# Banded attention with a mixture layer: PSUM tiles of one bank each, and GpSimd as the issuer of most later transfers

## The chip, the cores and the metric

The kernel runs on one core of one Trainium2 chip. The metric is the device time of one execution in microseconds (us). The kernel before took 714.76 us, the median of 3 runs (714.32 to 716.55). The profile is of one further execution, which took 713.8 us.

Five engines work side by side, each through its own list of instructions in a fixed order: PE (TensorE, matrix products), DVE (VectorE), ACT (ScalarE), POOL (GpSimd) and SP (SyncE, which here only issues transfers). An instruction starts when those before it in its own list are out of the way and the semaphores that it waits for have arrived. Products land in PSUM, which has eight banks of 512 fp32 numbers per partition.

## What is computed

Attention with a window and a few sink positions, then two dense layers with a gate between them, all in fp32:

```python
keep = is_sink | in_window                  # 4 sinks, a window of 128
scores = np.where(keep, scale * np.matmul(q, k.transpose(0, 1, 3, 2)), -1e9)
a = softmax(scores)
x = np.matmul(a, v)                         # 4 x 8 heads x 768 x 64
x = x.transpose(0, 2, 1, 3).reshape(3072, 512)
h = x @ w_in                                # 512 -> 2048
out = (h - np.tanh(h)) @ w_out              # 2048 -> 512
```

## The kernel before

**Tiling.** The 3072 tokens are cut into 12 chunks of 256. A chunk's attention is four units (a unit is two heads), so there are 48. A chunk's dense part is eight steps, one for each group of 256 hidden columns, so there are 96. Products are made in fp32r with operands split into a high and a low part, so that a product takes three passes (high by high, low by high, high by low).

**A unit.** The scores (L511, or L504 in the first 12 units) go into a pair of PSUM banks, one bank for each head. `merge` (L516 to L534) copies the sink columns into place under a mask (`copy_predicated`, L525) and then masks and finds the extreme of a row (L531). Exponentials and scales follow on ACT (L539, L565), sums on DVE (L559, L560), small copies for the sinks on POOL (L574 to L576). `turn` transposes the probabilities on PE into bank t (L599); ACT copies them out (L616, or L606 for the first chunk of a sequence), DVE writes a masked copy (L613), POOL masks the other (L619). `attend` transposes the sink columns into bank x (L640), ACT copies them (L647), and PE multiplies with the values (L656, L662) into banks x and t, from which ACT and DVE make the high and low part of x (L674, L678). Ahead of all that, `split` makes high and low parts of the keys (L469 on ACT, L474 on DVE) and of the queries (L479 on ACT, L482 on POOL).

**A step.** 24 products (L777) make two halves of h in one of two further PSUM buffers. The gate is tanh on ACT (L796) and a difference on DVE (L799). In chunks 3 and 4 and in the last step, high and low of it (L802, L805) go into 12 products with w_out (L847). In chunks 5 to 11 the second layer is one level of Strassen's scheme: sums on DVE (L810 to L812), high and low (L815 on ACT, L818 on DVE), and 21 products (L881) into seven accumulators that lie in the banks s0, s1, o0 and o1. At a chunk's end `gather` adds these up (L920 on ACT, L924 to L933 on DVE) and the result is stored (L938). `derive` (L964 to L1030) makes the summed weights for it during chunks 3 and 4. The last chunk's last step puts its products (L847) into banks t and x, which L953 adds.

**Weights.** w_in is spilled to a scratch in DRAM, `wscr`. From chunk 3 on each step reads its 1 MB of w_in again as four blocks into a ring of five buffers (`ring` and `spare`, L762). One part of w_out is put away in `kscr` and read back near the end (L742).

**Order.** No loop order is written down. Each piece of work is given to `Work.add` with an engine, an assumed duration, a due time, and the resources that it reads and writes; `Work.order` then runs a list scheduler over all of it, which picks, whenever an engine comes free, the ready piece with the earliest due time. The instructions of each engine are issued in that order. The due times come from constants (`PACE` for the distance of steps, `LEAD` for how far a chunk's attention lies ahead of its steps, `STREAM` for the ring loads, and others). The planner knows single banks (its resources are "s0", "s1", "o0", "o1", "t", "x"). The tiles of the language, which decide on what an instruction really waits, were three: `sbank`, `obank` and `txbank`, of two banks each.

**Transfers.** All of them are issued by SP, in one list.

Of the kernel before, what the change touches and what calls it, by code (L numbers as in the profile page):

```python
# [18 lines left out]
P = 128  # L19
# [213 lines left out]
def _banded(tc, qd, kp, vp, vs, masks, w_in, w_out, ident, pts, early, out):  # L233
    nc = tc.nc
    et = mybir.EngineType
    with ExitStack() as ctx:
# [26 lines left out]
        SLK, PAD, LATE, QP, KP, BP, LEAD3 = 0.0, 1.05, 65222.0, 1, 0, 1, 37045.0  # L263
# [56 lines left out]
        def load_qk(u):  # L320
# [34 lines left out]
            work.add("SP", 500, t, keys, (), [slots(u)[0], "seq k"], lands=800)  # L355
            work.add("SP", 1000, t, queries, (), [slots(u)[1], "seq q"], lands=600 if raw(u) else 1000)
# [3 lines left out]
        def load_v(cc):  # L360
            b, c = chunks[cc]
            first = max(0, 2 * c - 1)
            if c and chunks[cc - 1] == (b, c - 1):
                first = 2 * c
                if c:
                    vslot[cc, first - 1] = vslot[cc - 1, first - 1]
            new = range(first, 2 * c + 2)
            for i in new:
                vslot[cc, i] = ("v", len(vnew) % 3)
                vnew.append(i)  # L370

# [8 lines left out]
            work.add("SP", 500 * took, due_unit(4 * cc), values, (), [vslot[cc, i] for i in new] + ["seq v"],  # L380
                     lands=1000 * took)
# [111 lines left out]
        def scores(u, t):  # L493
# [4 lines left out]
            def products():  # L498
                both = obank if apart else sbank if cc <= SA else txbank
                ps = [both[:, h, :] for h in range(2)]  # L500
                sps[u, t] = both, ps
# [14 lines left out]
            def merge():  # L516
                both, ps = sps[u, t]
# [220 lines left out]
        def keep(back):  # L738
            for f in range(2):
                a = wt[1, NG - 1][:, :, f, (1 - f) * DM // 2 : (2 - f) * DM // 2].bitcast(F32)  # L740
                if back:
                    nc.sync.dma_start(a, kscr[f])  # L742
# [93 lines left out]
        def sums_of(n, cc, t):  # L836
            return (sbank, txbank, obank)[{1: 0, 2: 1, NCHUNK - 1: 1}.get(cc, 2)][:, t, :]

        def mm2(n, k):
# [16 lines left out]
            4: (sbank[:, 0, :HALF], 1), 3: (sbank[:, 0, HALF:], 0), 1: (obank[:, 1, :HALF], 2),  # L856
            2: (sbank[:, 1, :HALF], 3), 5: (sbank[:, 1, HALF:], 4),
            7: (obank[:, 0, :HALF], 6), 6: (obank[:, 0, HALF:], 5),
# [51 lines left out]
        def gather(n):  # L910
# [8 lines left out]
            def copy():  # L919
                nc.scalar.copy(v, pair(sbank[:, 0, :]))  # L920

            def add1():
                one = obank[:, 1, :HALF].unsqueeze(1).to_broadcast([P, 2, HALF])
                nc.vector.tensor_tensor(u, one, v, op=ALU.add)  # L924

            def add2():
                nc.vector.tensor_tensor(v, pair(sbank[:, 1, :]), v, op=ALU.add)
                for k in range(2):
                    nc.vector.tensor_tensor(u[:, k, :], u[:, k, :], sbank[:, 1, (1 - k) * HALF : (2 - k) * HALF], op=ALU.subtract)

            def add3():
                for k in (1, 0):
                    nc.vector.tensor_tensor(u[:, k, :], obank[:, 0, k * HALF : (k + 1) * HALF], u[:, k, :], op=ALU.add)  # L933
# [12 lines left out]
            if cc < NCHUNK - 1:  # L946
                for t in range(2):
                    work.add("SP", 500, d + 1000, lambda t=t: put(t), o, (), lands=1000)
                return

            def add4(t):
                part = four[:, 0::3, :] if t else four[:, 1:3, :]
                nc.vector.tensor_tensor(part, pair(txbank[:, t, :]), part, op=ALU.add)  # L953
# [172 lines left out]
        for n in range(NS):  # L1126
# [6 lines left out]
            if n:  # L1133
# [8 lines left out]
                if n - 1 == order.index((NCHUNK - 2, NG - 1)):  # L1142
                    work.add("SP", 1000, due_step(n + 2), lambda: keep(True), ["kept"], [("w", 1, NG - 1)], lands=2050)
# [214 lines left out]
```

## Time and profile before

| | |
|---|---|
| median of 3 runs | 714.76 us |
| profiled execution | 713.8 us |
| its span (first to last instruction) | 712.0 us |
| PE busy | 94% of the span |
| DVE busy | 77% |
| ACT busy | 58% |
| POOL busy | 25% |

The span is what the trace shows; 1.8 us of the execution lie around it. A busy share is an average over stages that differ: the first 80 us (loading, decoding weights, the first three chunks' attention), 80 to 200 us (plain steps of chunks 0 to 2), 200 to 360 us (chunks 3 and 4, with the derivation of Strassen's weights), 360 to 640 us (chunks 5 to 10 with attention beside them), and the rest. Where the trace gives a wait, it names what came last by semaphore.

### The profile page before, as it was taken

The numbers are of one execution on the slowest core, as the hardware profiler recorded it, in microseconds if no ns is written. First come the engines' busy times: TensorE is split into PE (matmuls) and PEld (weight loads), VectorE is DVE, ScalarE is ACT, GpSimd is POOL, SyncE is SP. The second block draws the span as 40 slices with busy tenths as digits, with TensorE's granted clock in tenths as the row PEclk, the third lists the DMA queues.
The fourth block names the chain that finished last, engine by engine and source line by source line (L and its number), as shares of the span: only waits on it lengthen the run. The fifth ranks groups of instructions, "written<-read, shape, count | busy, mean of one in ns | idle before, by whom it ended". The sixth has DMA issues, their size and how long they took to land.

```text
span 712.0 us, 14370 instructions
## 1 busy us (share of the span) xinstructions
PE 666.9 (94%) x5099; PEld 611.2 (86%) x5099; DVE 551.4 (77%) x1305; ACT 410.0 (58%) x1056; POOL 177.2 (25%) x287
## 2 busy tenths in 40 slices
PE   6788999999999997999999999999999998999896
PEld 5556899889988787889889889999999998999895
DVE  6777998964878898889878768877886876875554
ACT  5876333345876675656567557566565665663231
POOL 5332100001436464313222212223111231210000
PEclk9999999999999998999999999999999999999999
DMA  6769972432148665657857865866775775664761
GB/s 187 244 198 335 351 293 104 152 115 86 53 116 242 187 194 155 194 161 232 229 178 200 258 185 174 239 211 190 232 220 185 210 239 167 180 184 135 237 192 65
DMA packets 77485, 137.23 MB, mean 193 GB/s; under 512 B 8156, under 2 KB 28764, under 8 KB 77404
## 3 DMA queue, kind: packets, MB, share of 16 engines
q1 hardware_dynamic: 77404, 136.22, 62.0%
q8 instruction: 42, 0.69, 0.4%
q14 instruction: 39, 0.32, 0.1%
HBM read 120.98 MB, written 15.20 MB: 191 GB/s over the span
## 4 chain that ended last, share of the span: by engine, by line
PE 71%; DVE 10%; DMA 7%; ACT 6%; issue 2%; POOL 1%; SPq 0%; ACTq 0%; DVEq 0%
PE h L777 30%; PE sbank L881 10%; PE obank L881 7%; DMA ring<-wscr 6%; PE txbank L662 5%; PE obank L847 5%; PE txbank L847 3%; PE sbank L847 3%; PE txbank L511 3%; PE txbank L599 2%; DVE pt L613 2%; PE sbank L511 1%; ACT p L565 1%; PE txbank L656 1%; ACT pt L616 1%
## 5 line engine op out<-in xcount | busy, mean ns | idle before, releaser
L777 PE MATMUL h<-xh,ring 128*128 128x256 f32 x924 | 185.8, 282 | 8.6 <-DMA ring<-wscr 5.5
L777 PEld LDWEIGHTS h<-xh,ring 128*128 128x128 f32 x924 | 151.3, 190 | 10.9 <-DMA ring<-wscr 7.0
L777 PE MATMUL h<-xl,ring 128*128 128x256 f32 x462 | 129.0, 279 | 0.0
L796 ACT ACTIVATE gbuf<-h 128x512 f32<-128x512 f32 x96 | 57.3, 597 | 105.5 <-PE h L777 65.8
L482 POOL TENSOR_TENSOR q<-qraw,q 128x512 fp32r<-128x512 f32 x36 | 47.4, 1318 | 254.5 <-ACT q L479 254.5
L777 PEld LDWEIGHTS h<-xl,ring 128*128 128x128 f32 x462 | 87.6, 190 | 0.4
L539 ACT ACTIVATE p<-p,st 128x132 f32<-128x132 f32 x168 | 66.5, 398 | 26.8 <-DVE st L531 25.6
L815 ACT CAST ghbuf<-gbuf 128x896 fp32r<-128x896 f32 x55 | 51.9, 943 | 39.1 <-DVE gbuf L812 38.7
L777 PE MATMUL h<-xh,w 128*128 128x256 f32 x384 | 73.4, 281 | 0.0
L818 DVE TENSOR_TENSOR glbuf<-gbuf,ghbuf 128x896 fp32r<-128x896 f32 x55 | 61.2, 1112 | 15.2 <-ACT ghbuf L815 13.6
L777 PEld LDWEIGHTS h<-xh,w 128*128 128x128 f32 x384 | 60.8, 188 | 1.3 <-PE txbank L662 0.2
L565 ACT ACTIVATE p<-p,st 128x132 f32<-128x132 f32 x168 | 54.2, 394 | 4.3 <-DVE st L560 3.8
L474 DVE TENSOR_TENSOR ks<-kraw,ks 64x392 fp32r<-64x392 f32 x72 | 49.5, 687 | 5.6 <-ACT ks L469 3.0
L777 PE MATMUL h<-xl,w 128*128 128x256 f32 x192 | 53.5, 279 | 0.0
L847 PE MATMUL obank<-w,ghbuf 128*128 128x512 f32 x192 | 51.5, 399 | 1.4 <-ACT ghbuf L802 1.4
L799 DVE TENSOR_TENSOR gbuf<-h,gbuf 128x512 f32<-128x512 f32 x55 | 37.9, 689 | 18.8 <-ACT gbuf L796 18.3
L777 PE MATMUL h<-xh,spare 128*128 128x256 f32 x228 | 50.7, 285 | 0.2 <-DMA spare<-wscr 0.2
L619 POOL TENSOR_TENSOR pt<-pt,after 128x512 f32<-128x512 f32 x32 | 43.4, 1358 | 29.4 <-ACT pt L616 27.3
L613 DVE TENSOR_TENSOR pt<-txbank,below 128x512 f32<-128x512 f32 (+1 forms) x48 | 28.9, 602 | 26.8 <-ACT pt L616 9.7
L574 POOL CAST z<-p 128x16 fp32r<-128x16 f32 x42 | 11.5, 274 | 124.4 <-ACT p L565 119.2
L662 PE MATMUL txbank<-pt,v 128*64 128x128 f32 (+1 forms) x512 | 41.5, 315 | 0.0
L662 PEld LDWEIGHTS txbank<-pt,v 128*64 128x64 f32 x512 | 31.0, 137 | 11.8 <-issue 4.6
(157 smaller groups left out, 1620.8 us busy)
## 6 DMA issues: line engine op xcount, KB each, us to landing
ring<-wscr SPq DMA_DIRECT2D x231, 256.0 KB, 4.1
spare<-wscr SPq DMA_DIRECT2D x57, 256.0 KB, 4.1
qraw<-qd SPq DMA_DIRECT2D x36, 256.0 KB, 4.6
wraw<-w_in SPq DMA_DIRECT2D x16, 512.0 KB, 8.2
wraw<-w_out SPq DMA_DIRECT2D x16, 512.0 KB, 8.2
wscr<-w SPq DMA_DIRECT2D x16, 512.0 KB, 4.9
kraw<-kp SPq DMA_DIRECT2D x38, 196.0 KB, 3.9
v<-vp SPq DMA_DIRECT2D x27, 256.0 KB, 2.9
```

What stands on the lines that cost most here:

```text
L474: (nc.gpsimd if KP else nc.vector).tensor_tensor(k[o, h, :], t[r, :], k[r, h, :].bitcast(F32), op=ALU.subtract)
L482: (nc.gpsimd if QP else nc.vector).tensor_tensor(ql[u], qt[u], qh[u].bitcast(F32), op=ALU.subtract)
L539: nc.scalar.activation(e, e, AF.Exp, bias=st[u][:, j : j + 1], scale=-1.0, accum_out=st[u][:, 4 + j : 5 + j],)
L565: nc.scalar.activation(pr[u][:, j, :], pr[u][:, j, :], AF.Copy, scale=s[:, 8 + j : 9 + j])
L619: nc.gpsimd.tensor_tensor(w[:, :, 0, :], w[:, :, 0, :], after.unsqueeze(1).to_broadcast([P, 4, P]), op=ALU.mult)
L662: nc.tensor.matmul(xps[key][(p - p0) // 2][h * 64 : h * 64 + 64, p % 2, a:z], lhsT=vt[cc, i][:, hd : hd + D], rhs=rhs, start=False, stop=p ...
L777: nc.tensor.matmul(hps[n][:, f, :], lhsT=w, rhs=x, start=r == 0, stop=r == 11)
L796: nc.scalar.activation(g0, h(), AF.Tanh)
L815: nc.scalar.copy(ghbuf[:, n % 2], gbuf[:, 1:, :])
L818: nc.vector.tensor_tensor(glbuf[:, :7, :], gbuf[:, 1:, :], ghbuf[:, n % 2].bitcast(F32), op=ALU.subtract)
L847: nc.tensor.matmul(sums_of(n, cc, t), lhsT=a[:, f, t * P : (t + 1) * P], rhs=wt[1, g][:, (0, 1, 0)[i], f, :], start=first and not low and ...
L881: nc.tensor.matmul(acc, lhsT=a[:, b, :], rhs=factor(g, m, part % 2), start=g == 0 and part == 0 and m in (4, 1, 2, 7), stop=closes(n) and ...
```

## The change

Four things are changed.

1. The three PSUM tiles of two banks become six tiles of one bank. A `copy_predicated` over two banks becomes two, one per bank, each ahead of its own head's masking.
2. From chunk 4 on the values, from unit 12 on the keys and queries, the output stores of chunks 5 to 10, and the reload of `kscr` are issued by GpSimd: 104 transfers (36 of keys, 36 of queries, 18 of values, 12 stores, 2 of `kscr`). SP's list falls from 701 to 597 instructions.
3. `QP` goes from 1 to 0: the low part of the queries (L482, 36 instructions) is made by VectorE.
4. Eight constants of the planner change.

The instructions of PE are the same in number; VectorE gets 116 more (36 and 80).

```diff
-        sbank = ps.tile([P, 2, 512], F32, tag="s", name="sbank")
-        obank = ps.tile([P, 2, 512], F32, tag="o", name="obank")
-        txbank = ps.tile([P, 2, 512], F32, tag="tx", name="txbank")
-        tbank, xbank = txbank[:, 0, :], txbank[:, 1, :]
+        banks = {n: ps.tile([P, 512], F32, tag=n, name=n) for n in ("s0", "s1", "o0", "o1", "t", "x")}
+        sbank, obank, txbank = ((banks[a], banks[b]) for a, b in (("s0", "s1"), ("o0", "o1"), ("t", "x")))
+        tbank, xbank = txbank
...
-        SLK, PAD, LATE, QP, KP, BP, LEAD3 = 0.0, 1.05, 65222.0, 1, 0, 1, 37045.0
+        SLK, PAD, LATE, QP, KP, BP, LEAD3 = 0.0, 1.05, 65222.0, 0, 0, 1, 32490.0
...
-        FIRST, EARLY, PACE, LEAD = 45000.0, 4600.0, 7980.0, 43356.0
+        FIRST, EARLY, PACE, LEAD = 45000.0, 4600.0, 7895.0, 33530.0
...
-        HALF2, LAST = 8253.0, 6188.0
-        SPILL, STREAM, DEAR, DLATE = 36773.0, 5446.0, 120000.0, 17426.0
+        HALF2, LAST = 8807.0, 174.0
+        SPILL, STREAM, DEAR, DLATE = 25023.0, 6494.0, 120000.0, 31436.0
...
-                nc.sync.dma_start(kt[u], kp[b, p, :, 2 * c * TS : 2 * c * TS + KW])
+                (nc.sync if raw(u) else nc.gpsimd).dma_start(kt[u], kp[b, p, :, 2 * c * TS : 2 * c * TS + KW])
...
-                    nc.sync.dma_start(qt[u], src.rearrange("h d s -> d h s"))
+                    nc.gpsimd.dma_start(qt[u], src.rearrange("h d s -> d h s"))
...
-                    nc.sync.dma_start(vt[cc, i], vp[b, i * P : (i + 1) * P, :])
+                    (nc.sync if cc < 4 else nc.gpsimd).dma_start(vt[cc, i], vp[b, i * P : (i + 1) * P, :])
...
-                if kind > 0:
-                    nc.vector.copy_predicated(
-                        both[:, :, TS:WIN], above.bitcast(U32).unsqueeze(1).to_broadcast([P, 2, P]),
-                        both[:, :, :P],
-                    )
                 for h in range(2):
+                    if kind > 0:
+                        nc.vector.copy_predicated(ps[h][:, TS:WIN], above.bitcast(U32), ps[h][:, :P])
...
-                nc.sync.dma_start(out[r0 : r0 + P, :].rearrange("p (k c) -> p k c", k=2), src)
+                (nc.gpsimd if cc < NCHUNK - 1 else nc.sync).dma_start(
+                    out[r0 : r0 + P, :].rearrange("p (k c) -> p k c", k=2), src
+                )
```

Three places show how the lists change. The names at the end of a row are tiles, with a running number where there are several; line numbers of the kernel after are smaller by two to five than those of before.

The first place is the issuing of the last chunk's values. Before, SP issued them between ring loads:

```order
L377 DMA v_4_6932<-vp 128x512
L377 DMA v_5_6934<-vp 128x512
L762 DMA ring<-wscr 128x512
L762 DMA spare<-wscr 128x512
L343 DMA qraw_7028<-qd 128x2x256
L762 DMA ring<-wscr 128x512 x4
L762 DMA spare<-wscr 128x512
L762 DMA ring<-wscr 128x512
L334 DMA kraw_7107<-kp 128x392
```

In the kernel after, POOL issues the same values:

```order
L333 DMA kraw_7033<-kp 128x392
L377 DMA v_4_7049<-vp 128x512
L377 DMA v_5_7051<-vp 128x512
L342 DMA qraw_7140<-qd 128x2x256
L570 CAST z<-p_7086 128x2x8
L571 TENSOR_TENSOR z<-p_7086,z 128x2x8
L572 CAST z<-z 128x2x16
L333 DMA kraw_7197<-kp 128x392
L615 TENSOR_TENSOR pt<-pt,after 128x4x128
L934 DMA out<-wide 128x512
L934 DMA out<-wide 256x1x256
```

Keys, values, queries and stores have moved from among SP's ring loads to among POOL's sink copies (L570 to L572) and masked products (L615); SP there now issues ring and spare loads alone.

The second place is VectorE's list at the end of chunk 6, where `gather` reads the accumulators. Before:

```order
L799 TENSOR_TENSOR gbuf<-h_4980,gbuf 128x512
L810 TENSOR_TENSOR gbuf<-gbuf 128x256
L811 TENSOR_TENSOR gbuf<-gbuf 128x256
L812 TENSOR_TENSOR gbuf<-gbuf 128x128
L613 TENSOR_TENSOR pt<-txbank,below 128x4x128
L924 TENSOR_TENSOR wide<-obank,wide 128x2x256
L927 TENSOR_TENSOR wide<-sbank,wide 128x2x256
L929 TENSOR_TENSOR wide<-wide,sbank 128x256 x2
L933 TENSOR_TENSOR wide<-obank,wide 128x256 x2
L818 TENSOR_TENSOR glbuf<-gbuf,ghbuf 128x896
L525 COPY_PREDICATED txbank<-above,txbank 128x2x128
```

After, at the same place:

```order
L795 TENSOR_TENSOR gbuf<-h_5045,gbuf 128x512
L806 TENSOR_TENSOR gbuf<-gbuf 128x256
L807 TENSOR_TENSOR gbuf<-gbuf 128x256
L808 TENSOR_TENSOR gbuf<-gbuf 128x128
L920 TENSOR_TENSOR wide<-o_239,wide 128x2x256
L923 TENSOR_TENSOR wide<-s_237,wide 128x2x256
L925 TENSOR_TENSOR wide<-wide,s_237 128x256 x2
L929 TENSOR_TENSOR wide<-o_238,wide 128x256 x2
L525 COPY_PREDICATED t<-above,t 128x128
L527 ISA p_5117,st_5118<-t,mask 128x132
L527 ISA st_5118 128x1
L525 COPY_PREDICATED x<-above,x 128x128
```

The additions stand in the same order and now name one bank each (o_239 is o1, s_237 is s1, o_238 is o0); the masked copy before them (L613) is gone from here, and the predicated copy is halved and alternates with the masking (L527).

The third place is VectorE's list where the Strassen weights of group 6 are derived a second time (L985 to L1008 before, L983 to L1006 after). Before:

```order
L985 TENSOR_TENSOR wide<-w_6_1527 128x512
L799 TENSOR_TENSOR gbuf<-h_3627,gbuf 128x512
L613 TENSOR_TENSOR pt<-txbank,below 128x4x128
L810 TENSOR_TENSOR gbuf<-gbuf 128x256
L811 TENSOR_TENSOR gbuf<-gbuf 128x256
L812 TENSOR_TENSOR gbuf<-gbuf 128x128
L987 TENSOR_TENSOR wide<-wide,w_6_1527 128x512
L989 TENSOR_TENSOR wide<-wide,w_6_1527 128x512
L818 TENSOR_TENSOR glbuf<-gbuf,ghbuf 128x896
```

After:

```order
L983 TENSOR_TENSOR wide<-w_6_1554 128x512
L985 TENSOR_TENSOR wide<-wide,w_6_1554 128x512
L987 TENSOR_TENSOR wide<-wide,w_6_1554 128x512
L555 TENSOR_SCALAR st_3812<-st_3812 128x4
L556 RECIPROCAL st_3812<-st_3812 128x4
L482 TENSOR_TENSOR q_3840<-qraw_3593,q_3840 128x512
L1004 TENSOR_TENSOR w_6_1554<-wide,w_6_1554 128x256
L1006 SCALAR_TENSOR_TENSOR w_6_1554<-wide,w_6_1554 128x256
L474 TENSOR_TENSOR ks_3871<-kraw_3614,ks_3871 64x392 x2
```

The low part of the queries (L482) now stands in VectorE's list, and the three sums of the derivation follow one another.

On PE, the last product with the values of a chunk (L662) stood 1.5 to 2.75 steps ahead of the first step of that chunk in chunks 4 to 11; it now stands 0.75 to 2 steps ahead.

## Rows read from the trace of the kernel before

**Rows 1.** The busy time of each engine over the span, with its share and its number of instructions (PEld is the loading of weights into TensorE).
```profile
PE 666.9 (94%) x5099; PEld 611.2 (86%) x5099; DVE 551.4 (77%) x1305; ACT 410.0 (58%) x1056; POOL 177.2 (25%) x287
```
**Rows 2.** The span by stage: stretch and its length in us; busy time and (count) of PE, PEld, DVE, ACT and POOL; the granted clock of PE as a share of the full one; the DMA share; GB/s.
```profile
0.00:80.00 80.00, 63.80 (x386) 48.98 (x387) 60.32 (x210) 53.39 (x184) 29.19 (x78) 1.00 0.76 246
80.00:200.00 120.00, 119.36 (x778) 107.41 (x777) 95.71 (x158) 59.25 (x128) 13.77 (x21) 1.00 0.43 154
200.00:360.00 160.00, 151.54 (x1080) 135.22 (x1080) 139.63 (x322) 103.55 (x285) 66.53 (x84) 0.98 0.65 192
360.00:640.00 280.00, 269.21 (x2332) 259.79 (x2331) 217.18 (x550) 173.97 (x434) 66.27 (x104) 1.00 0.68 204
640.00:712.00 72.00, 62.99 (x532) 59.82 (x530) 38.52 (x69) 19.88 (x29) 1.46 (x1) 0.98 0.52 158
```
**Rows 3.** What PE waited for between 80 and 700 us: total in us, times, the longest.
```profile
PE h L777 <- DMA ring<-wscr: 5.5, 7, 1.8
PE sbank L881 <- DVE wide L929: 4.4, 5, 1.0
PE h L777 <- issue: 3.1, 1, 3.1
PE txbank L640 <- DVE pt L613: 2.4, 4, 1.0
...
PE txbank L640 <- ACT pt L616: 1.0, 1, 1.0
```
**Rows 4.** The same view for the first 80 us.
```profile
PE txbank L599 <- ACT zr L647: 3.9, 3, 1.6
...
PE txbank L599 <- DVE xl L678: 1.5, 3, 0.5
PE txbank L640 <- ACT pt L606: 1.0, 1, 1.0
```
**Rows 5.** What SP's queue waited for between 200 and 700 us, the same columns.
```profile
SPq L377 <- PE txbank L662: 27.4, 8, 5.4
SPq L343 <- POOL q L482: 25.2, 10, 5.9
SPq L334 <- DVE ks L474: 22.3, 21, 2.8
```
**Rows 6.** The timeline around one stop of PE at 601 us: start and duration in us, the instruction, and in brackets the idle time before it with its releaser. Rows of POOL, then SP, then PE.
```profile
596.30 1.29 POOL L482 TENSOR_TENSOR q<-qraw,q 128x512 fp32r<-128x512 f32 x1 [11.29 <-ACT q L479]
...
597.62 0.38 SPq L343 DMA_DIRECT2D qraw<-qd  x1
598.09 2.20 SPq L762 DMA_DIRECT2D ring<-wscr  x4
...
602.95 0.39 PE L777 MATMUL h<-xh,ring 128*128 128x256 f32 x1 [1.85 <-DMA ring<-wscr]
```
**Rows 7.** The timeline at the end of chunk 6, in the same form. Rows of DVE, then PE.
```profile
450.22 0.74 DVE L929 TENSOR_TENSOR wide<-wide,sbank 128x256 f32<-128x256 f32 x2
...
449.52 0.63 PE L511 MATMUL txbank<-ks,q 128*128 128x260 f32 x4
451.11 0.71 PE L881 MATMUL sbank<-edge,ghbuf 128*128 128x256 f32 x4 [0.96 <-DVE wide L929]
...
452.57 0.64 PE L881 MATMUL sbank<-w,ghbuf 128*128 128x256 f32 x4
```
**Rows 8.** Groups of instructions by line and shape over the whole span: out<-in with shapes, count, busy us, mean ns of one, idle time before them. The last row is from the view of one line and gives the least, the median and the greatest duration in ns.
```profile
L482 POOL TENSOR_TENSOR q<-qraw,q 128x512 fp32r<-128x512 f32 x36 | 47.4, 1318 | 254.5 <-ACT q L479 254.5
...
L474 DVE TENSOR_TENSOR ks<-kraw,ks 64x392 fp32r<-64x392 f32 x72 | 49.5, 687 | 5.6 <-ACT ks L469 3.0
...
L805 DVE TENSOR_TENSOR glbuf<-h,ghbuf 128x512 fp32r<-128x512 f32 x41 | 28.1, 685 | 2.5 <-ACT ghbuf L802 2.1
...
L810 DVE TENSOR_TENSOR gbuf<-gbuf 128x256 f32<-128x256 f32 x55 | 24.1, 438 | 1.8
...
L525 DVE COPY_PREDICATED txbank<-above,txbank 128x256 f32<-128x256 uint32 x44 | 18.7, 424 | 9.2 <-PE txbank L511 6.2 <-ACT gbuf L796 2.9
...
L812 DVE TENSOR_TENSOR gbuf<-gbuf 128x128 f32<-128x128 f32 x55 | 17.1, 312 | 1.9
...
L474 DVE TENSOR_TENSOR ks<-kraw,ks x72: 559/562/1418, 153.5 to 625.2; 64x392 fp32r<-64x392 f32 x72
```
**Rows 9.** The longest stop of PE after 80 us, on the timeline (a row of DVE, one of PE), and the stretch in which it lies, in the columns of rows 2.
```profile
280.31 0.68 DVE L805 TENSOR_TENSOR glbuf<-h,ghbuf 128x512 fp32r<-128x512 f32 x1
...
281.09 0.55 PE L777 MATMUL h<-xh,ring 128*128 128x256 f32 x1 [3.14 <-issue]
...
280.00:300.00 20.00, 18.91 (x108) 17.22 (x109) 15.55 (x43) 13.21 (x39) 4.89 (x6) 0.87 0.54 158
```
**Rows 10.** The timeline at the end, DVE.
```profile
705.61 1.29 DVE L953 TENSOR_TENSOR wide<-txbank,wide 128x512 f32<-128x512 f32 x2 [1.29 <-PE txbank L847]
```
**Rows 11.** L482 by stage: stretch, length, busy time of POOL with its count, granted clock, DMA share, GB/s.
```profile
200.00:360.00 160.00, 16.32 (x12) 0.98 0.65 192
360.00:640.00 280.00, 24.64 (x19) 1.00 0.68 204
```
**Rows 12.** L525 by stage, with the busy time and the count of DVE in the same columns.
```profile
200.00:360.00 160.00, 9.73 (x23) 0.98 0.65 192
360.00:640.00 280.00, 15.26 (x36) 1.00 0.68 204
```

More of the change, by code (lines that the diff above doesn't have):

```diff
@@ L354, in load_qk @@
                 work.add("POOL", 460, t - ZL, zeros, (), [slots(u)[1]])
-            work.add("SP", 500, t, keys, (), [slots(u)[0], "seq k"], lands=800)
-            work.add("SP", 1000, t, queries, (), [slots(u)[1], "seq q"], lands=600 if raw(u) else 1000)
+            e = "SP" if raw(u) else "POOL"
+            work.add(e, 500, t, keys, (), [slots(u)[0], "seq k"], lands=800 if raw(u) else 1000)
+            work.add(e, 1000, t, queries, (), [slots(u)[1], "seq q"], lands=600 if raw(u) else 1000)
         vslot, vnew = {}, []
@@ L376, in values @@
                     vt[cc, i] = vpool.tile([P, DM], F32, tag="v", name=f"v{cc}_{i}")
-                    nc.sync.dma_start(vt[cc, i], vp[b, i * P : (i + 1) * P, :])
+                    (nc.sync if cc < 4 else nc.gpsimd).dma_start(vt[cc, i], vp[b, i * P : (i + 1) * P, :])
             took = len(new)
-            work.add("SP", 500 * took, due_unit(4 * cc), values, (), [vslot[cc, i] for i in new] + ["seq v"],
+            work.add("SP" if cc < 4 else "POOL", 500 * took, due_unit(4 * cc), values, (), [vslot[cc, i] for i in new] + ["seq v"],
                      lands=1000 * took)
@@ L499, in products @@
                 both = obank if apart else sbank if cc <= SA else txbank
-                ps = [both[:, h, :] for h in range(2)]
-                sps[u, t] = both, ps
+                ps = sps[u, t] = both
                 for h in range(2):
@@ L516, in merge @@
             def merge():
-                both, ps = sps[u, t]
+                ps = sps[u, t]
                 if t == 0:
@@ L741, in keep @@
                 if back:
-                    nc.sync.dma_start(a, kscr[f])
+                    nc.gpsimd.dma_start(a, kscr[f])
                 else:
@@ L836, in sums_of @@
         def sums_of(n, cc, t):
[L837 removed]
+            return (sbank, txbank, obank)[{1: 0, 2: 1, NCHUNK - 1: 1}.get(cc, 2)][t]
         def mm2(n, k):
@@ L855, in _banded @@
         accs = {
-            4: (sbank[:, 0, :HALF], 1), 3: (sbank[:, 0, HALF:], 0), 1: (obank[:, 1, :HALF], 2),
-            2: (sbank[:, 1, :HALF], 3), 5: (sbank[:, 1, HALF:], 4),
-            7: (obank[:, 0, :HALF], 6), 6: (obank[:, 0, HALF:], 5),
+            4: (sbank[0][:, :HALF], 1), 3: (sbank[0][:, HALF:], 0), 1: (obank[1][:, :HALF], 2),
+            2: (sbank[1][:, :HALF], 3), 5: (sbank[1][:, HALF:], 4),
+            7: (obank[0][:, :HALF], 6), 6: (obank[0][:, HALF:], 5),
         }
@@ L919, in copy @@
             def copy():
-                nc.scalar.copy(v, pair(sbank[:, 0, :]))
+                nc.scalar.copy(v, pair(sbank[0][:, :]))
             def add1():
-                one = obank[:, 1, :HALF].unsqueeze(1).to_broadcast([P, 2, HALF])
+                one = obank[1][:, :HALF].unsqueeze(1).to_broadcast([P, 2, HALF])
                 nc.vector.tensor_tensor(u, one, v, op=ALU.add)
             def add2():
-                nc.vector.tensor_tensor(v, pair(sbank[:, 1, :]), v, op=ALU.add)
+                nc.vector.tensor_tensor(v, pair(sbank[1][:, :]), v, op=ALU.add)
                 for k in range(2):
-                    nc.vector.tensor_tensor(u[:, k, :], u[:, k, :], sbank[:, 1, (1 - k) * HALF : (2 - k) * HALF], op=ALU.subtract)
+                    nc.vector.tensor_tensor(u[:, k, :], u[:, k, :], sbank[1][:, (1 - k) * HALF : (2 - k) * HALF], op=ALU.subtract)
             def add3():
                 for k in (1, 0):
-                    nc.vector.tensor_tensor(u[:, k, :], obank[:, 0, k * HALF : (k + 1) * HALF], u[:, k, :], op=ALU.add)
+                    nc.vector.tensor_tensor(u[:, k, :], obank[0][:, k * HALF : (k + 1) * HALF], u[:, k, :], op=ALU.add)
             def put(t):
@@ L947, in gather @@
                 for t in range(2):
-                    work.add("SP", 500, d + 1000, lambda t=t: put(t), o, (), lands=1000)
+                    work.add("POOL", 500, d + 1000, lambda t=t: put(t), o, (), lands=1000)
                 return
@@ L952, in add4 @@
                 part = four[:, 0::3, :] if t else four[:, 1:3, :]
-                nc.vector.tensor_tensor(part, pair(txbank[:, t, :]), part, op=ALU.add)
+                nc.vector.tensor_tensor(part, pair(txbank[t][:, :]), part, op=ALU.add)
             def end():
@@ L1142, in _banded @@
                 if n - 1 == order.index((NCHUNK - 2, NG - 1)):
-                    work.add("SP", 1000, due_step(n + 2), lambda: keep(True), ["kept"], [("w", 1, NG - 1)], lands=2050)
+                    work.add("POOL", 1000, due_step(n + 2), lambda: keep(True), ["kept"], [("w", 1, NG - 1)], lands=2050)
                 if cc == 0 and g == NG - 1:
```

## The prediction

> **What bounds the kernel now.** I read the busy times first: PE is busy for 666.9 of 712.0 us, DVE for 551.4, POOL for 177.2 [rows 1]. So the end is set by PE's list plus its stops, and an edit pays only where it shortens a stop. The view by stage says where the stops are [rows 2]: PE lacks 80.0 − 63.8 = 16.2 us in the first 80, 0.6 in 80 to 200, 160.0 − 151.5 = 8.5 in 200 to 360, 280.0 − 269.2 = 10.8 in 360 to 640, and 9.0 in the last 72. The reader should also see that DVE is the second engine: 139.6 of 160 us (87%) in the third stage, 217.2 of 280 (78%) in the fourth. Third, PE's waits name who ends the stops [rows 3, 4]: ring loads, DVE's additions at the end of a chunk, copies out of banks t and x. Last, SP's waits show why a ring load comes late: the load ahead of it in the same list waits for a buffer [rows 5].
>
> **Part 1, one tile for each bank.** A wait by the old tile can hold an instruction for a reader of the other bank. The end of chunk 6 is the pattern [rows 7]: the four L881 products that start at 451.11 write bank s0 (accumulators 4 and 3), yet they waited 0.96 us for L929, which reads s1. The first products into s1 start at 452.57, when L929 is done. With six tiles that wait goes. It is there at five chunk ends, 4.4 us in all [rows 3]. Behind it stands only ACT's copy out of s0, which is earlier here. I take 4.0 (bounds 0 and 4.4).
>
> L640 transposes into bank x and waits for L613 and L616, which read bank t: 2.4 + 1.0 = 3.4 us [rows 3]. Behind it stand the small copies that make its input on POOL. I take 2.5 (0 to 3.4).
>
> In the first 80 us L599 (bank t) waits for L647 (bank x) and for L678, which there reads bank x, and L640 (bank x) for L606 (bank t): 3.9 + 1.5 + 1.0 = 6.4 us [rows 4]. Here true waits stand close behind, as the same copies and masks follow each other through both banks in every pair of units. I take about half, 3.0 (0 to 6.4).
>
> At the end both L953 additions wait for the last product, though the first reads bank t only [rows 10]. One of two, 1.29/2 = 0.64 us, can lie beside PE: I take 0.6 (0 to 0.64). Together part 1 gives 4.0 + 2.5 + 3.0 + 0.6 = 10.1 us.
>
> Its cost is on DVE: 80 predicated copies become 160. The shape of 128x256 takes 0.424 us; an addition falls from 0.438 to 0.312 us when its shape is halved [rows 8]. So I estimate a half copy at 0.424 − 0.126 = 0.298, and each edit at 2 × 0.298 − 0.424 = 0.172 us (bounds 0 and 0.424): 80 × 0.172 = 13.8 us over the kernel.
>
> **Part 2, transfers issued by GpSimd.** PE waits 5.5 us for ring loads, seven times [rows 3]. Rows 6 show the longest. L482 on POOL still reads the query buffer until 597.59; SP's query load stands at the head of its list until then, and the four ring loads behind it start at 598.09. PE stops for 1.85 us. With keys, queries and values out of SP's list, a ring load has nothing but ring loads ahead of it, and waits only for its own buffer. I take 4.5 of the 5.5 (0 to 5.5), leaving 1.0 for loads that queue behind other traffic: the DMA share is 0.65 to 0.68 already [rows 2].
>
> The Trainium skill, "DMA: Bandwidth & Descriptors", section "Issuing engines are not separate DMA queues", says that transfers run on the same DMA engines whoever issues them, and that issuing from several saves only the issuer's time. By that alone this term would be 0. The row speaks for more, since the loss there was a wait at the head of the issuer's list and not the transfer; I keep 0 as the rival "hidden anyway" below.
>
> On POOL the 104 issues come in, and no row of before has one. SP's issue of a query load takes 0.38 us [rows 6]; the nearest POOL instruction is L482 with 1.318 us [rows 8]. That bounds them by 104 × 0.38 = 40 and 104 × 1.318 = 137 us, in an engine that is idle for 712.0 − 177.2 + 47.4 = 582 us once L482 is gone. I take nothing on the path for the time itself. What can cost is order: 27.4 us of waits by value loads (up to 5.4 us each), 25.2 by query loads and 22.3 by key loads [rows 5] now stand at the head of POOL's list. Behind them are the sink copies that L640 needs and the masked products that L662 needs. I take 0, because the planner puts an issue where its buffer should be free, and keep the bound as a rival.
>
> **Part 3, L482 on DVE.** 36 instructions leave POOL, where one takes 1.318 us, and join DVE, where the same shape takes 0.685 [rows 8]: 36 × 0.685 = 24.7 us. Part comes back: L474 takes 0.687 in the mean but 0.562 in the median [rows 8], and I put the excess down to POOL instructions beside it, L482 among them. The whole excess is 72 × 0.125 = 9.0; I take half, 4.5 (0 to 9.0). DVE then has 551.4 + 13.8 + 24.7 − 4.5 = 585 us, 82% of the span: still under PE. By stage it is less even. In 200 to 360 it gets 12 × 0.685 [rows 11] + 23 × 0.172 [rows 12] = 12.2 us, and is busy for 151.8 of 160, 95%. In 360 to 640 it gets 19 × 0.685 + 36 × 0.172 = 19.2 us, 236.4 of 280, 84%. A 95% busy engine with a fixed order can't hide all. PE's longest stop, 3.14 us at 281 us [rows 9], ended just after DVE's L805, which started at 280.31 and frees an h buffer. I charge a third of 12.2, 4.0 (0 to 12.2), for the third stage, and 2.5 for the fourth (0 to 7 chunk starts × 0.685 = 4.8).
>
> **Part 4, constants.** They move due times and no instruction count. In the new order attention ends 0.75 to 2 steps ahead of its chunk, before 1.5 to 2.75. No row prices that; PE waited for no low part of x after 80 us, so the row nearest is 0. I take 0, with −2 to +3 for the range: 3 is about the stop of rows 9 once more. After that stop the granted clock was at its lower level for a time (1.2 instead of 2.4 GHz; 0.87 in the mean of 280 to 300 us [rows 9]), which is (1 − 0.87) × 20.00 = 2.6 us of full speed missing. I take no change there: the stop may vanish with the order, or be as long as before.
>
> **Sum.** Gains 10.1 + 4.5 = 14.6, costs 4.0 + 2.5 = 6.5: 8.1 us less than the 713.8 of the profiled execution, 705.7. The median of the runs is 714.76, 0.96 above that execution, so I predict 706.7.
>
> **Rivals.**
>
> *Hidden anyway.* The ring loads are late because the DMA engines are busy, so part 2 gives 0: 714.76 − 10.1 + 6.5 = 711.2. For it: the share of 0.68 in the fourth stage. Against it: rows 6, where the issue itself was late. 0.14.
>
> *GpSimd's list blocks.* A value load at its head waits up to 5.4 us [rows 5], and sink copies and masked products stand behind. It bites only if a buffer comes free later than the planner assumed. If that costs PE 1.2 us (of the up to 5.4) at each of the seven chunks from 5 on, it is 8.4 us, the whole gain: 714.76 − 8.1 + 8.4 = 715.1, no change. The Trainium skill, "SBUF — State Buffer", section "SBUF: two separate sides", adds a way: while some VectorE operations hold the port that it shares with GpSimd, GpSimd can't write the descriptors of its own transfers. No row of before shows such a transfer. L482's 1.318 against 0.685 us fits the two engines being in each other's way, and DVE will be at 82%. 0.14.
>
> *VectorE becomes the bound* (the slower side). Its place is the third stage and the starts of chunks 5 to 11: the whole 12.2 us of 200 to 360, and 4.8 at the chunk starts where the low part of x now comes later; and the freed waits of part 1 turn into waits for the same DVE instruction's late start, so that the gain is half, 7.3. 714.76 + 12.2 + 4.8 − 7.3 = 724.5. It decides from the point where DVE's idle time in the third stage, 160.0 − 139.6 = 20.4 us [rows 2], is no longer where PE can wait for it: 95% busy is near. Against it: PE itself is idle for 8.5 us there, and lengthens nothing until those are used. 0.14.
>
> *All of it, and the clock.* The stop at 281 us goes with the finer waits, giving 3.1 + 2.6 = 5.7 more: 701.0. 0.06.
>
> The forecast has 0.52.
>
> **How the numbers follow.** The forecast's own range takes its terms from the low to the high half of their bounds: 701 to 711. The blocked list reaches to 717, the DVE rival to 724.5. I cut that one and put the range at 698 to 718, which leaves about 0.15 above and 0.05 below. A measurement of this kernel tells about 0.3% from no change, 712.6 to 716.9. Faster than that: the forecast (0.52), all of it (0.06) and most of hidden anyway (0.10), 0.68. Within: the blocked list's larger part and the rest of hidden anyway, 0.15. Slower: the DVE rival and the blocked list's tail, 0.17.
>
> **What would show it.** Part 1: no wait of L877 (L881 before) on L925, and none of the sink transposes on the copies out of bank t; predicated copies of 128x128 near 0.30 us. Part 2: no wait of PE on the ring above 0.5 us, SP waiting for PE alone, key, query and value loads on POOL's queue. Part 3: DVE near 585 us, 90 to 97% in the third stage; L474's mean near 0.62. The forecast is wrong if PE waits for POOL's sink copies or masked products by more than 3 us in all, if it waits for DVE in the third stage by more than 12, or if its granted clock falls in a second place.

## The result, and the profile after

The changed kernel takes 698.96 us (median of 4 runs, 698.40 to 699.54) against 714.54 for the kernel before in the same comparison (4 runs): a ratio of 0.9778, 95% interval 0.9755 to 0.9800. It is 15.6 us faster; 8.1 were forecast. The time lies 1 us inside the low end of the range of 698 to 718. The profiled execution took 698.51 us, its span 696.7.

Busy times over the span of the changed kernel, to be read beside [rows 1]:

```profile
PE 665.7 (96%) x5099; PEld 612.2 (88%) x5099; DVE 571.9 (82%) x1421; ACT 412.8 (59%) x1056; POOL 202.2 (29%) x355
```

PE does the same work in the same busy time; what went is its idle time. By stage, in the columns of [rows 2]:

```profile
0.00:80.00 80.00, 69.64 (x423) 55.65 (x424) 67.17 (x229) 54.96 (x186) 33.18 (x82) 1.00 0.84 288
80.00:200.00 120.00, 120.00 (x809) 107.98 (x809) 96.68 (x180) 63.42 (x141) 18.45 (x32) 1.00 0.37 129
200.00:360.00 160.00, 150.92 (x1062) 135.07 (x1062) 142.11 (x350) 102.71 (x277) 67.62 (x102) 0.99 0.64 197
360.00:640.00 280.00, 276.09 (x2406) 266.07 (x2405) 234.36 (x610) 176.97 (x434) 80.10 (x138) 1.00 0.67 204
```

In the first 80 us PE has 423 matmuls behind it instead of 386, and in 360 to 640 it lacks 3.9 us instead of 10.8. In 200 to 360 it lacks 9.1 (before 8.5): there nothing was won. What PE waited for between 80 and 690 us, to be read beside [rows 3], and in the first 80 us, beside [rows 4]:

```profile
PE h L773 <- DMA ring<-wscr: 6.1, 11, 1.7
PE s L510 <- DVE st L527: 2.6, 2, 2.1
PE o L843 <- ACT ghbuf L798: 1.8, 2, 1.1
PE h L773 <- issue: 1.1, 1, 1.1
...
PE x L636 <- POOL z L572: 0.7, 1, 0.7
```
```profile
PE s L503 <- DMA qk<-qd: 2.3, 1, 2.3
PE t L595 <- ACT pt L602: 1.9, 3, 0.8
PE t L595 <- DVE pt L609: 1.3, 1, 1.3
```

The reader should see three things. The waits for a reader of the other bank are gone: no product waits for the additions at a chunk's end (L925, before L929), and the sink transposes (L636) do not wait for the copies out of bank t. What is left at bank t is true: L595 writes it, L602 and L609 read it. And the wait for the ring has not shrunk: 6.1 us, against 5.5 before, although SP's list now holds hardly anything but ring loads. One such stop, rows of SP and then PE (start, duration, instruction, idle time with its releaser):

```profile
549.40 3.26 SPq L758 DMA_DIRECT2D ring<-wscr  x4
...
549.09 0.28 PE L773 MATMUL h<-xh,ring 128*128 128x256 f32 x1
...
553.97 0.38 PE L773 MATMUL h<-xh,ring 128*128 128x256 f32 x1 [0.52 <-DMA ring<-wscr]
```

The product at 549.09 is the last on its ring block; it ends at 549.37, and the first of the four loads goes out at 549.40. Nothing stood ahead of it. The data are needed at 553.45 and used at 553.97, 4.6 us after the issue, where the median from issue to landing of ring loads is 4.1. In the 4.1 us from 549.37 to 553.45 PE used up the other four blocks of the ring, about the time that one load takes. That fewer other stops bring this about is not shown: the kernel below with the fewest stops waits 1.8 us for the ring (all three in the old order).

What the transfers cost POOL (groups by line: count, busy us, mean ns of one, idle time before them with its releasers):

```profile
L342 POOL DMA_DIRECT2D qraw<-qd x36 | 26.9, 748 | 231.5 <-DVE q L482 161.9 <-ACT p L561 40.2 <-DVE st L556 23.1
L333 POOL DMA_DIRECT2D kraw<-kp x36 | 20.5, 571 | 27.8 <-DVE ks L474 18.4 <-issue 4.2 <-ACT p L561 4.0
L377 POOL DMA_DIRECT2D v<-vp x18 | 9.8, 549 | 26.2 <-PE t L658 18.9 <-issue 7.0 <-PE t L595 0.3
L934 POOL DMA_DIRECT2D out<-wide x12 | 7.8, 653 | 23.9 <-DVE wide L929 23.9
...
L738 POOL DMA_DIRECT2D w<-kscr x2 | 1.5, 755 | 16.2 <-PE h L773 16.2
```

104 issues take 66.5 us, 0.55 to 0.76 each, inside the prediction's bounds of 40 and 137; POOL waits long for buffers, and after 80 us PE waits for POOL 0.7 us in all. On VectorE the groups that the prediction priced, beside [rows 8]:

```profile
L482 DVE TENSOR_TENSOR q<-qraw,q 128x512 fp32r<-128x512 f32 x36 | 25.2, 700 | 1.4 <-ACT q L479 1.3
...
L474 DVE TENSOR_TENSOR ks<-kraw,ks 64x392 fp32r<-64x392 f32 x72 | 43.3, 601 | 3.0 <-ACT ks L469 0.9
...
L525 DVE COPY_PREDICATED t<-above,t 128x128 f32<-128x128 uint32 x44 | 12.8, 292 | 5.1 <-PE t L510 4.7
```

A half copy takes 0.29 us (estimated 0.298), L482 0.700, and L474 fell from 0.687 to 0.601. DVE is busy for 571.9 us, 13 less than the sum of 585 said, and for 89% of the third stage, not 95%.

### The profile page after: what moved, and what is told of

It is laid out like the page before. It is cut to its first block, busy times and chain, and to the rows that moved or that the text cites. A ratio compares the mean times of both kernels' runs of the same rounds, so it can differ in the third digit from the quotient of the medians.

```text
span 696.7 us, 14472 instructions
## 1 busy us (share of the span) xinstructions
PE 665.7 (96%) x5099; PEld 612.2 (88%) x5099; DVE 571.9 (82%) x1421; ACT 412.8 (59%) x1056; POOL 202.2 (29%) x355
## 4 chain that ended last, share of the span: by engine, by line
PE 74%; DVE 10%; DMA 8%; ACT 3%; POOL 2%; issue 2%; SPq 0%; POOLq 0%; DVEq 0%; ACTq 0%
PE h L773 30%; PE s L877 10%; PE o L877 7%; DMA ring<-wscr 7%; PE o L843 6%; PE x L658 3%; PE s L843 3%; PE t L658 2%; PE t L595 2%; PE t L510 2%; PE t L843 2%; PE x L843 2%; PE x L510 2%; PE s L510 1%; PE s L503 1%
## 5 line engine op out<-in xcount | busy, mean ns | idle before, releaser
L342 POOL DMA_DIRECT2D qraw<-qd x36 | 26.9, 748 | 231.5 <-DVE q L482 161.9
L814 DVE TENSOR_TENSOR glbuf<-gbuf,ghbuf 128x896 fp32r<-128x896 f32 x55 | 61.9, 1125 | 17.3 <-ACT ghbuf L811 9.6
L843 PE MATMUL o<-w,ghbuf 128*128 128x512 f32 x192 | 50.7, 398 | 1.9 <-ACT ghbuf L798 1.8
L795 DVE TENSOR_TENSOR gbuf<-h,gbuf 128x512 f32<-128x512 f32 x55 | 37.9, 688 | 15.9 <-ACT gbuf L792 14.9
L615 POOL TENSOR_TENSOR pt<-pt,after 128x512 f32<-128x512 f32 x32 | 43.7, 1367 | 20.5 <-ACT pt L612 20.4
L474 DVE TENSOR_TENSOR ks<-kraw,ks 64x392 fp32r<-64x392 f32 x72 | 43.3, 601 | 3.0 <-ACT ks L469 0.9
L609 DVE TENSOR_TENSOR pt<-t,below 128x512 f32<-128x512 f32 (+1 forms) x48 | 28.9, 601 | 18.2 <-ACT pt L612 8.4
L795 DVE TENSOR_TENSOR h<-h,gbuf 128x512 f32<-128x512 f32 x41 | 28.5, 694 | 16.2 <-ACT gbuf L792 16.0
L843 PEld LDWEIGHTS o<-w,ghbuf 128*128 128x128 f32 x192 | 33.8, 188 | 8.4 <-ACT ghbuf L798 2.5
L773 PEld LDWEIGHTS h<-xh,spare 128*128 128x128 f32 x228 | 39.1, 189 | 1.4 <-issue 1.2
```

The source lines that it names most:

```text
L474: (nc.gpsimd if KP else nc.vector).tensor_tensor(k[o, h, :], t[r, :], k[r, h, :].bitcast(F32), op=ALU.subtract)
L615: nc.gpsimd.tensor_tensor(w[:, :, 0, :], w[:, :, 0, :], after.unsqueeze(1).to_broadcast([P, 4, P]), op=ALU.mult)
L773: nc.tensor.matmul(hps[n][:, f, :], lhsT=w, rhs=x, start=r == 0, stop=r == 11)
L795: nc.vector.tensor_tensor(g0 if strassen(n) else h(), h(), g0, op=ALU.subtract)
L814: nc.vector.tensor_tensor(glbuf[:, :7, :], gbuf[:, 1:, :], ghbuf[:, n % 2].bitcast(F32), op=ALU.subtract)
L843: nc.tensor.matmul(sums_of(n, cc, t), lhsT=a[:, f, t * P : (t + 1) * P], rhs=wt[1, g][:, (0, 1, 0)[i], f, :], start=first and not low and ...
```

## The experiments

The change has four parts: the tiles with the halved copies (S), the transfers (T), L482 on VectorE (Q), and the constants (C). T, Q and C are inputs of the planner, so each of them also makes another order of all engines' lists. S is not: with it the lists of PE and ScalarE are those of before, and VectorE's has the halved copies as its only difference. All ratios below are to the kernel before, with 95% intervals.

**Each part alone.** The edits are the lines of the change shown above, for T with the planner's entry for the engine, as here:

```diff
-            work.add("SP", 500, t, keys, (), [slots(u)[0], "seq k"], lands=800)
+            e = "SP" if raw(u) else "POOL"
+            work.add(e, 500, t, keys, (), [slots(u)[0], "seq k"], lands=800 if raw(u) else 1000)
```

> Before with the six single-bank PSUM tiles and the halved predicated copies alone. Theory 1 (the tiles were worth more than my 10.1 us, because the false waits of the first 80 us go whole): 702 to 705 us, with the first dense steps some 6 us earlier, as in the changed kernel. Theory 2 (the excess comes from the planner's constants): 707 to 710 us, first steps 3 us earlier.

> Before with the 104 transfers issued by GpSimd alone. Theory 1 (the ring loads were late behind other transfers in SP's list): 709 to 711 us, PE's waits for the ring about 1 us. Rival (PE's ring waits are those of busy DMA engines): 714 to 716 us, ring waits still 4 us or more.

> Before with the low part of the queries made by VectorE alone. By the prediction's charge: 715 to 719 us. Rival (POOL's slow L482 held up the query buffer and VectorE's key parts, so that its move pays): 709 to 713 us.

> Before with the eight planner constants alone. Theory 1: 712 to 716 us. Theory 2 (the excess comes from them): 705 to 709 us.

Measured: S 696.57 us (0.9768, 0.9752 to 0.9785), T 726.66 (1.0196, 1.0174 to 1.0218), Q 722.52 (1.0118, 1.0101 to 1.0136), C 719.10 (1.0070, 1.0053 to 1.0088). No expectation held: S is below both ranges, T and C above both, and Q slower than even the prediction's charge. The tiles alone give all of the gain and a little more (their interval overlaps that of the whole change). The other three, each alone, make the kernel slower by 5 to 14 us, though in the changed kernel they cost hardly anything together. In the first 80 us of S, as in the changed kernel, no wait for a reader of the other bank is left; the longest that are left, besides the start:

```profile
PE t L594 <- ACT pt L601: 1.7, 3, 0.8
PE s L502 <- DVE st L526: 1.6, 1, 1.6
```

In 200 to 360 us of T, PE waits for VectorE and ScalarE where the kernel before hardly did; neither of the two longest names a transfer of POOL:

```profile
PE obank L848 <- ACT wide L1040: 4.7, 1, 4.7
PE sbank L512 <- DVE st L532: 4.5, 3, 2.9
```

**Each part taken back.** The same edits, undone one at a time in the changed kernel.

> The changed kernel with the two-bank tiles put back. Theory 3 (transfers, L482 and constants each cost what they cost alone, 13.1 + 8.9 + 5.5 us, and the finer waits are what makes them cheap): 730 to 742 us. Rival (the three belong together and mend each other, and the tiles only add their 17 us): 713 to 719 us.

> The changed kernel with all transfers issued by SP again. Theory 3: 696 to 700 us. Rival (the constants and L482 on VectorE need the transfers on GpSimd): 703 to 710 us. By the prediction's term for the ring: 703 us.

> The changed kernel with the low part of the queries made by POOL again. Theory 3: 695 to 699 us. Rival (with transfers on POOL, POOL's list can't take L482 too): 703 to 712 us.

> The changed kernel with the constants of before. Theory 3: 696 to 701 us. Rival (the constants are what makes transfers on GpSimd and L482 on VectorE pay): 705 to 715 us.

Measured: without S 715.36 us (1.0017, 0.9995 to 1.0038), without T 711.02 (0.9942, 0.9923 to 0.9962), without Q 707.97 (0.9892, 0.9845 to 0.9938), without C 707.78 (0.9889, 0.9844 to 0.9934). Theory 3 fell: T, Q and C together change the kernel with two-bank tiles by nothing that can be measured, where their sum alone would be 27 us. And any one of the three missing from the changed kernel costs 8 to 12 us, by the ratios. So they are not additive, and the tiles are not what makes them cheap. No S, no Q and no C fall into their rival's range, no T 1 us above it. This left the order itself as the suspect: every kernel that is slow here mixes one kernel's constants with the other's engines.

**The same parts in an unchanged order.** T and Q were tried again with the planner left as it was, so that every instruction stays at its place in the order and only the issuing engine differs (shown for T: the line of the queries, as one of five):

```diff
-                    nc.sync.dma_start(qt[u], src.rearrange("h d s -> d h s"))
+                    nc.gpsimd.dma_start(qt[u], src.rearrange("h d s -> d h s"))
```
```diff
-                (nc.gpsimd if QP else nc.vector).tensor_tensor(ql[u], qt[u], qh[u].bitcast(F32), op=ALU.subtract)
+                nc.vector.tensor_tensor(ql[u], qt[u], qh[u].bitcast(F32), op=ALU.subtract)
```

> Before with the 104 transfers issued by GpSimd, but with the planner still counting them as SP's, so that PE, VectorE and ScalarE keep the order of before, and GpSimd has each transfer where SP had it. Theory 4 (the 13 us of only_T come from another order of all engines, not from who issues): 710 to 716 us. Rival (GpSimd as issuer costs by itself): 722 to 730 us.

> Before with the low part of the queries (L482) issued to VectorE, at the place in time that the planner gave POOL, so that no other instruction changes place. Theory 4 (the 9 us of only_Q come from another order): 711 to 717 us. Rival (24.7 us more on VectorE cost by themselves): 720 to 726 us.

Measured: T 712.08 us (0.9974, 0.9955 to 0.9994), Q 710.85 (0.9963, 0.9947 to 0.9979). Each is a small gain instead of a loss of 8 to 14 us. The same instructions on the same engines, in two orders, so differ by 0.0222 (16 us) for T and by 0.0155 (11 us) for Q. Both gain at the ring; of T and then of Q, over the whole span (before: 5.5 us, 7 times [rows 3]):

```profile
PE h L777 <- DMA ring<-wscr: 2.9, 5, 1.2
```
```profile
PE h L777 <- DMA ring<-wscr: 3.1, 5, 1.1
```

With T the ring loads no longer stand behind a query load that waits. With Q the subtraction takes 0.69 us instead of 1.32, and SP waits a little less for the query buffer (before 25.2 us, at most 5.9 at a time [rows 5]):

```profile
SPq L343 <- DVE q L482: 22.1, 11, 5.2
```

That this alone makes Q's gain is not shown. VectorE's busy time rises by 6.9 us only (551.4 to 558.3), though 36 × 0.69 = 24.7 us of instructions joined it.

**The order alone.** `LEAD` was moved by 0.3 us either way, with the work of every engine as before:

```diff
-        FIRST, EARLY, PACE, LEAD = 45000.0, 4600.0, 7980.0, 43356.0
+        FIRST, EARLY, PACE, LEAD = 45000.0, 4600.0, 7980.0, 43056.0
```

> Before with LEAD at 43056 in place of 43356, a change of 0.3 us in the attention's due times, which by itself moves nothing that matters but makes the list scheduler choose another order in many places. Theory 4 (an order other than the one the constants were chosen with costs 5 to 13 us whatever the cause): 719 to 728 us. Rival (orders are equivalent, and it was the kind of change that cost): 712 to 716 us.

> Before with LEAD at 43656, 0.3 us the other way. Theory 4: 719 to 728 us. Rival: 712 to 716 us.

Measured: 721.46 us (1.0095, 1.0061 to 1.0129) for the shorter lead and 715.50 (1.0008, 0.9987 to 1.0030) for the longer. The two differ in how much they changed. In a comparison of the lists of PE as the kernels build them, the shorter lead moves some 660 of about 5000 instructions (T alone some 530, Q 490, C 970), the longer 10. So a change that does nothing but reorder costs 6.8 us, about as much as C or Q alone, and one that reorders little costs nothing. How much is moved does not set the price: the changed kernel without S moves some 1040 and costs 0.0017. My expectation for the longer lead was wrong because I took the size of the step for the size of the change. With the shorter lead PE meets scores whose operands are late, which in the kernel before took 0.9 us in this stretch (the first row); waits of 80 to 700 us:

```profile
PE sbank L511 <- DVE ks L474: 5.9, 5, 4.0
PE h L777 <- DMA ring<-wscr: 4.9, 6, 2.4
PE txbank L511 <- DVE st L531: 2.8, 3, 1.2
```

**The tiles, taken apart.** The same code with some pairs kept as tiles of two banks (here s and o, so that t and x alone are single), the other way round, and with all three kept, which leaves the halved copies alone:

```diff
-        sbank, obank, txbank = ((banks[a], banks[b]) for a, b in (("s0", "s1"), ("o0", "o1"), ("t", "x")))
+        def pairs_of(a, b, tag, two):
+            if two:
+                w = ps.tile([P, 2, 512], F32, tag=tag, name=tag)
+                return w[:, 0, :], w[:, 1, :]
+            return ps.tile([P, 512], F32, tag=a, name=a), ps.tile([P, 512], F32, tag=b, name=b)
+
+        sbank, obank, txbank = (pairs_of(*z) for z in (("s0", "s1", "sbank", 1), ("o0", "o1", "obank", 1), ("t", "x", "txbank", 0)))
```

> Before with single-bank tiles for t and x alone; s and o stay two-bank tiles, the predicated copies are halved everywhere. If the 17 us of only_S are mostly false waits between banks t and x: 700 to 705 us, first dense steps some 7 us earlier. If the chunk ends (s) and the scores (s, o) carry most: 706 to 712 us.

> Before with single-bank tiles for s0, s1, o0 and o1; t and x stay one two-bank tile, the predicated copies are halved everywhere. If t and x carry most: 708 to 713 us. If the chunk ends and scores do: 702 to 707 us.

> Before with two-bank tiles and the predicated copies halved alone. VectorE gets 13.8 us by the prediction's estimate. If VectorE hides it: 713 to 716 us. If it lies on the path (and so_one paid it): 717 to 722 us.

Measured: t and x single 703.18 us (0.9860, 0.9831 to 0.9889), s and o single 714.80 (1.0002, 0.9983 to 1.0021), copies alone 722.35 (1.0116, 1.0082 to 1.0150). The second lies above both ranges expected for it, which had left out the price of the copies. In ratios the copies cost 0.0116, about 8.3 us; against that, t and x save 0.0256 (18.3 us) and s and o 0.0114 (8.1 us). The two together would be 0.9746 and S has 0.9768: within their intervals they add up. What the copies cost once the banks are single can't be measured apart, since a copy can't span two tiles; so 0.0232 (16.6 us) is what single banks gain with their copies, and 0.0348 (25 us) what they gain against the copies alone. In the changed kernel's order S is worth as much: 0.9778 against 1.0017 without it, 0.0239. The copies' 8.3 us are most of what they add on VectorE, 46.7 − 33.8 = 12.9 us (46.7 is the sum of these rows, 33.8 that of all stages in the view of [rows 12]):

```profile
L529 DVE COPY_PREDICATED txbank<-above,txbank 128x128 f32<-128x128 uint32 x88 | 25.8, 293 | 10.0 <-PE txbank L514 6.1 <-ACT gbuf L796 2.2
...
L529 DVE COPY_PREDICATED sbank<-above,sbank 128x128 f32<-128x128 uint32 x48 | 14.0, 292 | 8.5 <-PE sbank L514 7.7
...
L529 DVE COPY_PREDICATED obank<-above,obank 128x128 f32<-128x128 uint32 x24 | 6.9, 288 | 1.9 <-PE obank L507 1.3
```

With t and x single, the waits at the chunk ends stay as they were, as they should:

```profile
PE sbank L881 <- DVE wide L929: 4.4, 5, 1.0
```

**All three in the old order.** The tiles, the transfers on GpSimd and L482 on VectorE, with the planner and its constants as before.

> Single-bank tiles, transfers issued by GpSimd and L482 on VectorE, all in the order that the planner made for the kernel before. Theory 4 (each of the three pays a little or nothing lost when the order stays): 696.6 less 2.2 less 3.5, so 689 to 693 us, below both kernels. Rival (the two gains were the same ring waits of PE, or VectorE is now too full): 694 to 698 us.

Measured: 694.17 us (0.9721, 0.9694 to 0.9747), faster than the changed kernel (0.9755 to 0.9800) and than S (0.9752 to 0.9785), whose intervals it just clears. It falls into the rival's range: T and Q add 0.0047, about 3.4 us, not 5.7. The rows fit the first half of the rival: T and Q alone each took some 2.5 of 5.5 us off the waits for the ring, and here these are 1.8, where S has 5.1. Whether VectorE, now busy for 572.1 us, is too full was not tried apart. The changed kernel has the same tiles and the same engines, and its order costs 0.0057, 4.1 us, against this one. PE's longest wait here after the first 80 us, and that for the ring:

```profile
PE h L772 <- issue: 3.5, 1, 3.5
...
PE h L772 <- DMA ring<-wscr: 1.8, 3, 1.1
```

Where the time goes can be followed by the start of each dense step's first product, taken from each trace; the table gives how much later (+) or earlier (−) in us than in the trace of before:

| step | changed | S | copies | T | shorter lead | S, T, Q in the old order |
|---|---|---|---|---|---|---|
| 6 | −6.6 | −7.6 | +0.5 | +0.2 | −0.1 | −7.2 |
| 24 | −6.9 | −8.4 | +1.2 | +1.4 | −0.1 | −8.4 |
| 40 | −8.2 | −10.0 | +1.5 | +9.6 | +2.4 | −7.7 |
| 56 | −5.5 | −15.4 | +1.2 | +10.9 | +6.7 | −11.8 |
| 72 | −8.1 | −17.4 | +2.7 | +12.6 | +4.6 | −15.0 |
| 95 | −14.9 | −16.7 | +5.6 | +12.3 | +9.2 | −19.0 |

Steps 24 to 39 are chunks 3 and 4, 40 on the Strassen chunks. The changed kernel and S part between 40 and 56, where the changed kernel gives back 2.7 us and S gains 5.4; the changed kernel makes most of it up again by the end.

## Why the prediction was right and wrong

The sign, and that PE's false waits were the place, were right; the gain was twice the forecast, and it did not come as the sum said. By the runs, the ratio's 0.0222 (15.9 us) is 16.6 us from the tiles with their copies and 3.4 from T and Q in the old order, less 4.1 for the new order. The time lies in the range because errors met there: the tiles gave more than was taken, and the order, taken at 0, gave part of it back. All three parts in the old order take 694.17 us, below the range.

- **Part 1, the tiles: the step that failed.** It was put at 10.1 us of gain. Against the copies alone the tiles gave 25 us by the ratios (18 for t and x, 8 for s and o), and with the copies' cost in it 16.6. The term for the first 80 us was put at 3.0; 6.6 were found in the changed kernel by step 6 and 8.1 in S against the copies. I halved it because true waits "stand close behind"; in the runs nearly all of it came. A wait of L656 (bank x) for L613 (bank t) in the first 80 us, 2.5 us, I had left out of the rows and the sum; it too is gone from the list of the changed kernel. The 6.4 us of the three rows and these 2.5 make 8.9. The other terms, 7.1 together, were too small as well: between step 6 and step 95 S gains 14.2 us more on the copies. Why they gave twice their rows is open. I read it so that each false wait that goes makes the next copy and the next mask start earlier, and the true waits move too; no run shows that apart.
- **The copies' cost.** 13.8 us on DVE were well estimated (12.9 measured). That VectorE hides most of it was wrong: with tiles of two banks 8.3 us of it reach the end. The charge of 6.5 for copies and L482 together falls short by about 2 us for the copies alone.
- **Part 2, the transfers.** In the old order they gave 0.0026, 1.9 us, for the 4.5 taken; in the changed kernel the ring waits are as long as before. The reading of rows 6 was right, as T in the old order shows: the ring waits fall to 2.9 us, to 1.8 with all three. That they are 6.1 in the changed kernel goes with its order, in which a load can be late with nothing ahead of it (the stop at 553.97); the prediction left 1.0. "What would show it" named a ring wait above 0.5 us as the sign against, and 1.7 us occurred. That POOL's own time and POOL's blocked list would cost nothing held in the old order, where T gains with both. The Trainium skill, "DMA: Bandwidth & Descriptors", section "Issuing engines are not separate DMA queues", agrees for the queries, which land 4.6 us after their issue from SP and from GpSimd alike; the stores landed later from GpSimd (last section). What was saved here was not the issuer's own time, which that section names, but the wait at the head of SP's list.
- **Part 3, L482.** Charged within the 6.5; in the old order it gains 0.0037, 2.6 us, where a cost was forecast. Its 24.7 us of durations were right and yet added 6.9 us of busy time: of L474's excess of 9.0 us, of which I took half, 8.2 came back. The prediction's 95% for the third stage was 89%. The VectorE rival is out.
- **Part 4, the constants.** "I take 0, with −2 to +3" was wrong as a way of pricing. C alone costs 5.0 us; T and Q alone cost 14 and 8, through the order, and 0.3 us of lead costs 6.8. In the change itself the new order costs 4.1 us against the old one, above the 3 of the range. That the four parts can be summed at all was an assumption that I had not stated. T, Q and C together nearly cancel: 0.0017 in the ratio with two-bank tiles and 0.0010 with single ones.
- **The clock.** The stop of [rows 9] is there again in every kernel with the order of before, 3.0 to 3.5 us long. In the changed kernel a shorter one of 2.1 us stands near its place, at 272 us (L510 for L527), and the granted clock falls less: 0.91 and 1.00, where before it was 0.96 and, in [rows 9], 0.87 (means of 260 to 280 and of 280 to 300 us; those under 1.00 lie in part at the lower level, 1.2 instead of 2.4 GHz). So the rival that asked for all of it was right in part on that stop. That its time (701.0) is 2 us from the result is luck.

The wait of L656 in the kernel before, and the two stretches in the changed kernel, in the columns of [rows 2]:

```profile
PE txbank L656 <- DVE pt L613: 2.5, 2, 1.3
```
```profile
260.00:280.00 20.00, 17.79 (x110) 15.74 (x109) 18.33 (x39) 11.70 (x32) 10.95 (x16) 0.91 0.64 196
280.00:300.00 20.00, 20.00 (x135) 18.21 (x134) 17.59 (x51) 14.57 (x41) 6.46 (x10) 1.00 0.62 198
```

Why a given order is slow stays open. The traces name the waits (scores before their keys, products before a gate), but that the planner's assumed durations or the tiles' waits cause them was not tried.

## What to carry to other kernels

Give each PSUM bank a tile of its own if different engines read the banks at different times, and count the false waits in the list in full: those that the prediction counted sum to 4.4 + 3.4 + 6.4 + 0.6 = 14.8 us, 17.3 with the one left out, and S gained 16.6 with the cost of its copies in it. Where a planner sets the order, every edit is two edits: price the work with the order held, and price the order with a change that does nothing else. Parts that were set together must be tried together and apart before any of them is kept; here the fastest kernel tried takes the tiles and the two moves, and leaves the constants alone.

## What I had not expected of the hardware

An instruction that joined VectorE added much less to its busy time than it lasts: 24.7 us of L482 joined it in the old order, and 6.9 came on top. The sum of the durations rose by only 11.2 us, since others got shorter, and 4.3 us more of it lie beside a neighbour. L474 alone, whose work is the same, gave back 8.2 us. Its mean was 0.687 us before and is 0.573 with Q in the old order, where L482 is gone from POOL:

```profile
L474 DVE TENSOR_TENSOR ks<-kraw,ks 64x392 fp32r<-64x392 f32 x72 | 41.3, 573 | 3.1 <-ACT ks L469 0.9
```

With T in the old order, where L482 is still on POOL, it is 0.681.

Loads issued by GpSimd landed about as soon as those issued by SP (medians of 4.5, 3.7 and 3.0 us for queries, keys and values with T in the old order, before 4.6, 3.9 and 2.9). The stores at a chunk's end and the reload of `kscr` did not: T in the old order has 4.8 and 5.3 us, where before the stores of the same line had 3.6, as far as their landings are in the trace, and the reload 3.6. In the changed kernel, with VectorE busy for 82% of the time, they take 5.3 and 5.2:

```profile
out<-wide POOLq DMA_DIRECT2D x12, 256.0 KB, 5.3
w<-kscr POOLq DMA_DIRECT2D x2, 256.0 KB, 5.2
```

That VectorE holds up GpSimd's descriptors, as the Trainium skill's "SBUF — State Buffer", section "SBUF: two separate sides", has it for some operations, would fit the stores and not the loads; no run here tells whether it is the cause.
